# Chunks of 64 instead of 48, both batches of a chunk as one pair, and inverses of 32-row halves, in a delta-rule attention followed by two MLPs

## The chip, the cores and the metric

The kernel runs on one core of one Trainium2 chip. The metric is the device time of one execution in microseconds (us). The engines are named as the profile names them: PE is TensorE's matmul, PEld its weight load, DVE is VectorE, ACT is ScalarE, POOL is GpSimd, SP is SyncE, which here only issues DMAs. `L492` is line 492 of the kernel before.

## The reference

For each of 4 batches and 8 heads, a state of 40 x 40 runs over 768 tokens; then every token (320 values, the 8 heads side by side) goes through two MLPs. Cut to what matters:

```python
for t in range(S):                                   # 768 tokens, per batch and head
    y[t] = einsum(r[t], state)                       # read before the update
    Sa = einsum(state, a[t])
    state = state * w[t] - outer(Sa, b[t]) + outer(v[t], k[t])
x = y.transpose(...).reshape(3072, 320)
x = x / sqrt(mean(x*x) + 1e-6) * rms_g
x = (silu(x @ w_gate) * (x @ w_val)) @ w_out         # 320 -> 1536 -> 320
h = x @ w_in                                         # 320 -> 2048
out = (h - tanh(h)) @ w_out2                         # 2048 -> 320
```

## The kernel before, in words

**Attention in chunks.** The recurrence is computed in chunks of C = 48 tokens. A unit is one chunk of one batch, all 8 heads of it (as 4 x 2); there are 64 units. Units alternate between the two batches of a pair (G = 2), so two consecutive units are independent and each unit depends on the one two places before it. For each unit, in order:

- the p stage (`emit_p`): two scans and a reciprocal on DVE for the running products of w, then three multiplications on POOL (some on DVE at the start), L245 to L252. Its results go to memory (`sp`) and are loaded again as `kl` and `Q`.
- `m` (L268): the products of the chunk's a and b, evicted by ACT, stored to memory (`md`).
- the inverse of the unit triangular matrix I + M of each head: for most units in groups of 8 by `inverse`, 47 steps of a multiplication (L308) and an addition (L310), each step cut between POOL (its first rows) and DVE; for the first two groups by `inverse_halves` on 24-row halves (L335, L338), which `join_halves` puts together with three products (L369, L373, L377). The results go to memory (`td`, `th`) and come back as `tt`.
- `rhs` (L492), `u` (L506, the solve: the inverse times the right-hand side), `kb` (L447, a transpose of the next unit's keys), `d` (L519, the state's change), `ut` (L554, a transpose of u), `z` (L563, with a mask on DVE, L565), `mak` (L469) and `s` (L544, a transpose of the state), and for each pair of units `y` (L585, L587), `e` (L456, a transpose of the decay) and the RMS norm. `x2` (L607) transposes the finished rows of x.

**The MLPs.** The weights come as words of 64 bits and are split into two single-precision parts by `split_words`: per piece two instructions on ACT (L160, L167), five on DVE (L161, L162, L163, L165, L166) and two on POOL (L170, L171); 48 pieces for the first MLP (6 chunks of 8), 40 for the second. MLP 1 runs in 12 blocks of 256 tokens; each block has 12 steps f of 128 hidden columns: two `up` products of 8 matmuls (L635, gate and value), evictions on ACT and DVE, a split into a high and a low part on ACT and POOL (L662, L663), and `down` with 6 matmuls (L640 to L642). MLP 1 is mixed into the attention: between the attention's steps `moe(R * MO[i])` puts in as many pieces of MLP 1 as a credit allows (R is about 0.8 for each of 7 places in a unit), if a block's 256 tokens are done. MLP 2 follows in 6 blocks of 512 tokens with 16 steps each.

**What sets the order.** The program text gives each instruction a priority number (`step` advances it, `later` puts work behind), and a scheduler turns these into one fixed order on each engine. Every engine then works through its list in order and waits where an operand isn't there. SP issues nearly all DMAs in one list. `warm(n)` puts n bf16 matmuls without a use into the PE list. Most buffers of a unit exist twice (`NR = 2`; `RU` and `SN` three times), and the PE results rotate through three banks (`bank`).

**Start.** The first 16 units have hand-made places: MPOS, P8, JOINS, EXTRA, RATES and other tables set when their p stage, `m`, joins and the first weight pieces come.

## Time and profile before

| | |
|---|---|
| time of 3 runs, median (lowest to highest) | 1452.94 us (1450.84 to 1456.26) |
| the profiled execution's own time | 1455.73 us |
| its span in the trace | 1454.0 us |
| granted PE clock, mean over the span | 0.923 of full |
| first `rhs` (unit 0) | 65.8 us |
| first matmul of MLP 1 (L635) | 168.5 us |
| `rhs` of the last unit | 1002.0 us |
| first matmul of MLP 2 | 1081.5 us |

How to read it: the attention with MLP 1 mixed in fills the span from about 170 to 1012 us, the rest of MLP 1 and MLP 2 the time behind that. A row of a group gives the line, the engine, the tiles, the shapes and a count, then the busy time in us and the mean duration of one in ns, and behind the next bar the idle time of the engine ahead of it, with what released it. In the windows view a row is a stretch: its length, then for each engine its busy time and in brackets its number of instructions, then the granted PE clock (1.00 is full), the DMA engines' share and GB/s. The trace counts an fp32 product twice (two passes), so `x8` in the order of instructions stands as 16 in the trace; a transpose counts once.

### The profile page before, as it was taken

How to read it: one execution, taken by the hardware profiler on the slowest of the kernel's cores; microseconds unless marked ns; L12 is line 12 of the kernel's file. 1: busy time of each engine (PE TensorE's matmuls, PEld its weight loads, DVE VectorE, ACT ScalarE, POOL GpSimd, SP SyncE). 2: the span in 40 equal slices, each digit the busy share in tenths (PEclk: the TensorE clock that was granted, in tenths of full speed). 3: DMA queues.
4: the chain of work that ended last, by engine and by line, in shares of the span. 5: the costliest groups of instructions: out<-in, count | busy, mean ns of one | idle time of the engine just before them, and what ended most of it. 6: DMA issues, size and time to landing. Idle time of an engine off the chain costs nothing.

```text
span 1454.0 us, 38826 instructions
## 1 busy us (share of the span) xinstructions
PE 1310.8 (90%) x15090; PEld 1167.2 (80%) x15090; DVE 882.8 (61%) x2156; ACT 606.9 (42%) x1655; POOL 799.1 (55%) x1397
## 2 busy tenths in 40 slices
PE   2797798898998998998999989999887999999998
PEld 2676687787887888887888878899776898989988
DVE  8678898886957846845954957333869322222221
ACT  1244454443444453444445445444434433333332
POOL 6475786886855845854862864112757433333333
PEclk9976766779999999898999999999999999999999
DMA  7687576556455455455455243331322100010000
GB/s 175 144 239 181 145 192 166 153 135 145 122 135 132 117 146 137 120 135 133 107 140 118 64 120 101 81 75 49 103 76 87 35 17 18 23 35 24 1 19 19
DMA packets 224872, 151.44 MB, mean 104 GB/s; under 512 B 135600, under 2 KB 199632, under 8 KB 223920
## 3 DMA queue, kind: packets, MB, share of 16 engines
q1 hardware_dynamic: 197608, 131.96, 36.1%
q10 hardware_dynamic: 27080, 16.98, 4.2%
q8 instruction: 120, 1.97, 0.6%
q14 instruction: 64, 0.52, 0.1%
HBM read 111.23 MB, written 37.65 MB: 102 GB/s over the span
## 4 chain that ended last, share of the span: by engine, by line
PE 55%; DVE 23%; DMA 8%; POOL 6%; issue 4%; ACT 2%; SPq 1%; DVEq 0%; POOLq 0%; ACTq 0%
PE ups L635 22%; PE acc L640 6%; PE acc L642 5%; PE acc L641 5%; DVE arena L308 3%; DVE arena L310 3%; PE bank L563 2%; DVE fa L163 2%; DMA arena<-md 2%; DVE raw L166 2%; DVE fa L161 2%; PE bank L554 1%; PE gapped L519 1%; PE bank L506 1%; PE bank L469 1%
## 5 line engine op out<-in xcount | busy, mean ns | idle before, releaser
L635 PE MATMUL ups<-xh,w1c 128*128 128x256 f32 x1440 | 259.0, 313 | 16.7 <-DVE hf L659 9.1
L1152 POOL TENSOR_TENSOR hl<-th,hh 128x512 fp32r<-128x512 f32 x96 | 124.9, 1301 | 208.2 <-ACT hh L1151 203.3
L635 PEld LDWEIGHTS ups<-xh,w1c 128*128 128x128 f32 x1440 | 205.2, 204 | 29.1 <-DVE hf L659 11.1
L1148 DVE TENSOR_TENSOR th<-ups,th 128x512 f32<-128x512 f32 x96 | 66.3, 691 | 233.1 <-ACT th L1147 233.1
L663 POOL TENSOR_TENSOR hl<-hf,hh 128x256 fp32r<-128x256 f32 x144 | 117.4, 815 | 150.9 <-ACT hh L662 147.4
L635 PE MATMUL ups<-xl,w1c 128*128 128x256 f32 x864 | 158.6, 295 | 0.0
L635 PEld LDWEIGHTS ups<-xl,w1c 128*128 128x128 f32 x864 | 132.8, 204 | 0.0
L308 POOL TENSOR_TENSOR tmp<-arena 128x88 f32<-128x88 f32 (+45 forms) x282 | 108.2, 384 | 40.3 <-DMA arena<-md 23.9
L310 POOL TENSOR_TENSOR arena<-arena,tmp 128x88 f32<-128x88 f32 (+45 forms) x282 | 113.1, 401 | 16.7
L308 DVE TENSOR_TENSOR arena<-arena 128x182 f32<-128x182 f32 (+27 forms) x234 | 98.7, 422 | 32.0 <-POOL tmp L308 20.9
L1147 ACT ACTIVATE th<-ups 128x512 f32<-128x512 f32 x96 | 57.2, 596 | 130.4 <-PE ups L635 130.4
L657 DVE SCALAR_TENSOR_TENSOR th<-th,ups 128x256 f32<-128x256 f32 x144 | 59.5, 413 | 77.6 <-ACT th L656 76.8
L635 PE MATMUL ups<-yh,w2c 128*128 128x512 f32 x360 | 103.1, 397 | 2.9 <-DVE th L1148 2.9
L640 PE MATMUL acc<-w1c,hh 128*128 128x320 f32 x288 | 103.6, 360 | 0.1
L662 ACT CAST hh<-hf 128x256 fp32r<-128x256 f32 x144 | 58.4, 406 | 99.8 <-DVE hf L659 98.1
L310 DVE TENSOR_TENSOR arena<-arena 128x182 f32<-128x182 f32 (+27 forms) x234 | 93.3, 399 | 4.8
L642 PE MATMUL acc<-w1c,hl 128*128 128x320 f32 x288 | 92.6, 321 | 1.2 <-POOL hl L663 1.2
L656 ACT ACTIVATE th<-ups 128x256 f32<-128x256 f32 x144 | 55.2, 383 | 92.1 <-PE ups L635 83.2
L641 PE MATMUL acc<-w1c,hh 128*128 128x320 f32 x288 | 91.9, 319 | 0.0
L1151 ACT CAST hh<-th 128x512 fp32r<-128x512 f32 x96 | 59.5, 620 | 75.2 <-DVE th L1148 62.6
L640 PE MATMUL acc<-w2c,hh 128*128 128x320 f32 x288 | 86.9, 312 | 2.7 <-ACT hh L1151 2.7
L641 PE MATMUL acc<-w2c,hh 128*128 128x320 f32 x288 | 87.3, 312 | 0.0
(175 smaller groups left out, 3238.2 us busy)
## 6 DMA issues: line engine op xcount, KB each, us to landing
arena<-in_abkw_dram SPq DMA_DIRECT2D x48, 314.0 KB
RU<-in_vr_dram SPq DMA_DIRECT2D x64, 234.0 KB
sp<-arena ACTq DMA_DIRECT2D x40, 313.6 KB
kl<-sp SPq DMA_DIRECT2D x60, 156.0 KB
Q<-sp SPq DMA_DIRECT2D x60, 156.0 KB
raw<-in_w_out_dram SPq DMA_DIRECT2D x28, 320.0 KB
arena<-md SPq DMA_DIRECT2D x12, 576.0 KB
pl<-in_abkw_dram SPq DMA_DIRECT2D x16, 314.0 KB
```

What stands on the lines that cost most here:

```text
L308: eng.tensor_tensor(out=tv, in0=T[:, r0:r1, s:s + 1].to_broadcast([128, n, wd]), in1=M[:, s:s + 1, s + 1:C].to_broadcast([128, n, wd]), op ...
L310: eng.tensor_tensor(out=T[:, r0:r1, s + 1:C], in0=T[:, r0:r1, s + 1:C], in1=tv, op=ALU.add)
L635: PE.matmul(ps, lhsT=l, rhs=r[:, :n], start=i == 0, stop=i == 7)
L640: PE.matmul(acc[t][:, :DM], lhsT=hh[:, c], rhs=oh, start=f == 0, stop=False)
L641: PE.matmul(acc[t][:, :DM], lhsT=hh[:, c], rhs=ol, start=False, stop=False)
L642: PE.matmul(acc[t][:, :DM], lhsT=hl[:, c], rhs=oh, start=False, stop=f == nf - 1)
L657: DVE.scalar_tensor_tensor(out=th, in0=th, scalar=1.0, in1=ps[:, 0], op0=ALU.add, op1=ALU.mult)
L662: ACT.copy(hh, hf)
L663: POOL.tensor_tensor(out=hl, in0=hf, in1=hh, op=ALU.subtract)
L1148: DVE.tensor_tensor(out=th, in0=ps, in1=th, op=ALU.subtract)
L1151: ACT.copy(hh, th)
L1152: POOL.tensor_tensor(out=hl, in0=th, in1=hh, op=ALU.subtract)
```

## The change

C is 64 and the work item is a pair: both batches of one chunk, 24 pairs of 128 tokens, so that one `rhs` or `u` row of the order now has 16 products instead of 8, and a finished pair is one tile of 128 rows of x. What is different part by part:

- **Inverse.** Only the two 32-row halves on the diagonal are inverted, 31 steps each, always with one engine for a group: the first group (pairs 0, 1) on DVE, the second (2, 3), the third (4 to 7) and all later groups of four pairs on POOL. `inverse_halves`, `join_halves` and the joins' products are gone.
- **Solve.** `u` multiplies by the two inverted halves, of which the upper half is kept; `w` multiplies the upper half by the coupling block (`MX`, loaded from `md`), DVE subtracts it from the right-hand side `RS`, and `u2` multiplies again for the lower half.
- **Buffers.** One each of Q, VS, UV, RU, RS, TT, MX, EP and `kl`; `turn` rotates two PE banks beside `solve` and `gapped`.
- **Eviction and transposes.** `ut` and `s` are now products with the identity. The right-hand side is evicted half by ACT, half by DVE.
- **Weights.** `NRAW` 4 to 3, the split's scratch `fa` 4 to 2. The first two chunks of MLP 1's weights are split from the end of the first inverse on, chunks 2 to 5 after the last instruction of the third inverse.
- **MLP 1's place.** `moe(RATE)` with RATE = 2.1 at 9 places in a pair; ahead of `x2` a loop puts in what is left of the block before. Until the first block has begun, `warm(8)` stands there.
- **Output.** Each tile of 128 rows goes out in two DMAs of 64 rows.

The core of the diff:

```diff
-C = 48
+C = 64
+HC = C // 2
-GROUPS = [(0, 4), (4, 8)] + [(g, g + 8) for g in range(8, NU, 8)]
+GROUPS = [(0, 2), (2, 4)] + [(g, g + 4) for g in range(4, NP, 4)]
-NRAW = 4
+NRAW = 3
-RATE = 0.80
+RATE = 2.1
...
-        for s in range(C - 1):
-            nr, wd = s // jm + 1, C - 1 - s
-            for eng, r0, r1, buf in ((POOL, 0, min(nr, SPLIT), tmp), (DVE, SPLIT, nr, arena)):
...
+        for s in range(HC - 1):
+            nr, wd = s // jm + 1, HC - 1 - s
+            eng.tensor_tensor(out=tv, in0=T[:, :nr, s:s + 1].to_broadcast([128, nr, wd]),
                               in1=M[:, s:s + 1, s + 1:HC].to_broadcast([128, nr, wd]), op=ALU.mult)
+            lastd[0] = eng.tensor_tensor(out=T[:, :nr, s + 1:HC], in0=T[:, :nr, s + 1:HC], in1=tv, op=ALU.subtract)
...
+    def emit_u(p):
+                    PE.matmul(sol[r, w, q], lhsT=TT[r, w, q], rhs=RS[r, w, q], start=True, stop=True)
+        for s in range(2):
+            ACT.copy(UV[0:HC, :, s], sol[64 * s:64 * s + HC])
+    def emit_w(p):
+                    PE.matmul(tv[64 * s:64 * s + C, w, q], lhsT=MX[0:C, s, w, q], rhs=UV[0:C, w, s, q], start=True, stop=True)
+        DVE.tensor_tensor(out=RS, in0=RS, in1=tv, op=ALU.subtract)
+    def emit_u2(p):
+                    PE.matmul(sol[r, w, q], lhsT=TT[r, w, q], rhs=RS[r, w, q], start=True, stop=True)
+        for s in range(2):
+            ACT.copy(UV[HC:C, :, s], sol[64 * s + HC:64 * s + C])
...
+            i0 = inverse(0, DVE, M0, T0, fp)
+            i1 = inverse(1, POOL, M1, T1, fp)
+            i2 = inverse(2, POOL, M2, T2, fp)
...
+            run(i0)
+            first_w = lastd[0]
+            load_t(0)
+            emit_rhs(0)
+            warm(WARM0)
+            run(i1)
+            for u in range(12, 16):
+                emit_p(u, fp, POOL)
+                spill_p(u, SP)
+                if u % 2:
+                    emit_m(u // 2, fp)
+        with tc.issue_after(first_w.ins):
+            prep1(range(EARLY1), w1a)
+        later(2, run, i2)
+        last_t = lastd[0]
...
+        for p in range(NP + 1):
+            if p == 1:
+                with tc.issue_after(last_t.ins):
+                    prep1(range(EARLY1, KF1 // 2), w1p)
+            if now:
+                if p:
+                    emit_rhs(p)
+                    load_q(p + 1)
+            if p:
+                emit_y(p - 1)
+            moe(RATE)
+            if now:
+                emit_u(p)
+                moe(RATE)
+                emit_w(p)
+                    emit_kb(p + 1, 0)
+                moe(RATE)
+                emit_u2(p)
+                    emit_kb(p + 1, 1)
+                moe(RATE)
+                emit_d(p)
+                emit_ut(p)
+            if p:
+                while begun[0] < (p - 1) // 2 - 1 or (mlp and begun[0] == (p - 1) // 2 - 1):
+                    piece()
+                emit_x2(p - 1)
+            moe(RATE)
```

In this loop MLP 1's pieces can only come where a block's two pairs are done, and the credit and the loop put the 24 `up` products of a block where the order shows.

Three places in the order. First, PE's list around the start of the first solve. Before, with `rhs` of the first two units, the first join (L369) and, after 8 warming matmuls, `u` of unit 0:

```order
L492 MATMUL bank<-VS_209,Q_213 48x40 x8
L492 MATMUL bank<-VS_210,Q_214 48x40 x8
L369 MATMUL bank<-idn,mt 24x24 x16
...
L506 MATMUL bank<-rs_1133,arena 48x40 x8
L373 MATMUL bank<-mt 24x24 x16
```

Now `rhs` of pair 0 (L392) has 60 warming matmuls (L284) behind it, then come `m` of pairs 6 and 7 (L243), 8 warming matmuls, and `u` of pair 0 (L403):

```order
L392 MATMUL turn_137<-VS,Q 64x40 x16
L284 LDWEIGHTS wz
L284 MATMUL wps<-wz 128x256
...
L243 MATMUL turn_136<-po 64x64 x16
L243 MATMUL turn_137<-po 64x64 x16
...
L403 MATMUL solve<-RS,TT 64x40 x16
```

The `m` products of pairs 6 and 7, for which units 12 to 15 must have gone through their p stage, now stand ahead of the first solve; on POOL's list the p stage of units 12 to 15 stands behind the whole second inverse, among whose 62 instructions the POOL parts of the first 18 weight pieces are mixed.

Second, DVE's list at the same place. Before, the first masks of z (L565) alternate with the weight split (L161 to L166):

```order
L565 TENSOR_TENSOR z<-bank,msk 96x384
L161 TENSOR_SCALAR fa<-fa 128x256
L565 TENSOR_TENSOR z<-bank,msk 96x384
L162 TENSOR_SCALAR fa<-fa 128x256
L163 SCALAR_TENSOR_TENSOR fa<-raw,fa 128x256
L165 TENSOR_SCALAR raw<-fa 128x256
```

Now 18 pieces of the weight split (L138 to L143) and the p stage of units 12 to 15 stand ahead of the subtraction (L414) that pair 0's solve needs; here the end of that row:

```order
L142 TENSOR_SCALAR raw<-fa 128x256
L143 SCALAR_TENSOR_TENSOR raw<-raw 128x256
L214 SCALAR_TENSOR_TENSOR sx<-pl,z_151 104x260
L217 RECIPROCAL zr<-sx 104x4
L218 SCALAR_TENSOR_TENSOR po<-pl,zr 104x260
L214 SCALAR_TENSOR_TENSOR sx<-pl,z_151 104x260
L217 RECIPROCAL zr<-sx 104x4
L218 SCALAR_TENSOR_TENSOR po<-pl,zr 104x260
L414 TENSOR_TENSOR RS<-RS,turn_136 128x320
```

The subtraction moved behind all of these.

Third, PE's list in the steady part. Before, in a unit from `u` (L506) to `ut` (L554), with `down` and `up` of MLP 1 (L640 to L642, L635) beside them:

```order
L506 MATMUL bank<-rs,tt 48x40 x8
L447 MATMUL bank<-idn,kl 96x104 x4
L640 MATMUL acc_7539<-w1c_934,hh 128x320
L641 MATMUL acc_7539<-w1c_934,hh 128x320
L642 MATMUL acc_7539<-w1c_934,hl 128x320
L640 MATMUL acc_7540<-w1c_934,hh 128x320
L641 MATMUL acc_7540<-w1c_934,hh 128x320
L642 MATMUL acc_7540<-w1c_934,hl 128x320
L519 MATMUL gapped<-UV_211,kb 40x40 x8
L554 MATMUL bank<-idn,UV_211 40x48 x8
L635 MATMUL ups<-xh,w1c_1033 128x256 x5
```

Now, in every even pair: `u` (L403), `w` (L413), `kb` (L358), `u2` (L421), `kb`, `d` (L433), `ut` (L468), `x2` (L518), and only then `up` (L537):

```order
L403 MATMUL solve<-RS,TT 64x40 x16
L413 MATMUL turn_136<-UV,MX 64x40 x16
L358 MATMUL turn_137<-idn,kl 128x104 x4
L421 MATMUL solve<-RS,TT 64x40 x16
L358 MATMUL turn_136<-idn,kl 128x104 x4
L433 MATMUL gapped<-UV,kb 40x40 x16
L468 MATMUL turn_137<-idn,UV 40x64 x16
L518 MATMUL turn_136<-idn,XS 128x128 x3
L537 MATMUL ups<-xh,w1c_878 128x256 x5
L537 MATMUL ups<-xl,w1c_878 128x256 x3
```

In the even pairs the MLP pieces that stood between these steps are behind `x2` of the pair before it; in the odd pairs they still stand between the steps.

More of the change, by code (lines that the diff above doesn't have):

```diff
@@ L444, in emit_kb @@
+    def emit_kb(p, w):
+        bk = kl_t[p][w]
         t = bank()
@@ new lines, in wkv_chunks__then__gated_mlp__then__tanh_mlp_kernel, with some2 @@
+        todo = []
+        def some2():
+            if not w2:
+                tasks2.extend(early2())
+            with tc.issue_after(gate[0].ins), tc.issue_after(gate_act[0].ins):
+                while raw2:
+                    later(PRE2, split_words, *raw2.pop(0))
+            while tasks2 and len(raw2) < 2:
+                rows, *rest = tasks2.pop(0)
+                raw2.append((later(PRE2, fetch64, rows, rest[0]), *rest))
+        held = []
+        for p in range(NP + 1):
+            now, more, n = p < NP, p + 1 < NP, p + LOOKP
+            if p == 1:
+                for u in range(2 * KEEP):
+                    po_t.pop(u)
```

1081 lines of the change are left out of this document (404 added, 677 removed).

## The prediction, made before the changed kernel ran

> **What bounds the kernel now.** First the page: the busy time, the clock in 40 slices and the chain of work that ended last.
>
> ```profile
> PE 1310.8 (90%) x15090; PEld 1167.2 (80%) x15090; DVE 882.8 (61%) x2156; ACT 606.9 (42%) x1655; POOL 799.1 (55%) x1397
> PEclk9976766779999999898999999999999999999999
> PE 55%; DVE 23%; DMA 8%; POOL 6%; issue 4%; ACT 2%; SPq 1%; DVEq 0%; POOLq 0%; ACTq 0%
> PE ups L635 22%; PE acc L640 6%; PE acc L642 5%; PE acc L641 5%; DVE arena L308 3%; DVE arena L310 3%; PE bank L563 2%; DVE fa L163 2%; DMA arena<-md 2%; DVE raw L166 2%; DVE fa L161 2%; PE bank L554 1%; PE gapped L519 1%; PE bank L506 1%; PE bank L469 1%
> ```
>
> PE is busy for 90% of the span, but at a low clock in the first fifth, and DVE, with weight splits and inverses, holds 23% of the chain. So the span has parts with different limits; the windows view shows them (PE, PEld, DVE, ACT, POOL, then the clock).
>
> ```profile
> 0.00:60.00 60.00, 24.31 (x314) 19.83 (x315) 48.82 (x161) 8.94 (x21) 31.11 (x74) 1.00 0.71 168
> 60.00:120.00 60.00, 57.21 (x894) 47.13 (x891) 39.54 (x98) 27.82 (x76) 41.76 (x57) 0.74 0.77 201
> 240.00:300.00 60.00, 51.56 (x695) 44.91 (x695) 53.01 (x123) 26.66 (x79) 46.05 (x80) 0.70 0.54 141
> 300.00:420.00 120.00, 112.46 (x1577) 100.72 (x1577) 91.82 (x243) 51.69 (x159) 91.62 (x222) 0.92 0.54 131
> 1160.00:1278.00 118.00, 118.00 (x664) 106.40 (x663) 28.26 (x44) 42.47 (x76) 41.19 (x32) 1.00 0.08 25
> ```
>
> Until 300 us DVE has the most work that counts and PE runs at about 0.7 of its clock; then PE sets the pace. The rate of the attention comes from `rhs`, 16 records a unit: its line, and its records in two stretches.
>
> ```profile
> L492 PE MATMUL bank<-VS,Q x1024: 213/216/303, 65.8 to 1002.3; 112*48 112x40 f32 x166, 104*48 104x40 f32 x5
> 307.50:660.00 352.50, 14.28 (x400) 11.30 (x400) 0.94 0.53 131
> 660.00:1003.00 343.00, 14.87 (x416) 11.79 (x416) 0.96 0.41 101
> ```
>
> The two stretches hold 51 starts, the first at 307.5, the last at 1002: 50 steps in 694.5 us, 13.9 us a unit, or (128/48 units) 37.1 us for 128 tokens. Below, all is counted for 128 tokens, now one pair.
>
> **PE's work, before and after.** The timeline of PE at full clock gives the price of each step, from its start to the start of the next row.
>
> ```profile
> 307.50 0.56 PE L492 MATMUL bank<-VS,Q 112*48 112x40 f32 x16
> 307.99 0.86 PE L635 MATMUL ups<-xh,w1c 128*128 128x256 f32 x5
> 309.04 0.76 PE L635 MATMUL ups<-xh,w1c 128*128 128x256 f32 x5
> 310.09 0.56 PE L506 MATMUL bank<-rs,tt 48*48 48x40 f32 x16
> 310.58 0.56 PE L447 MATMUL bank<-idn,kl 104*96 104x104 f32 x4
> 310.92 0.39 PE L640 MATMUL acc<-w1c,hh 128*128 128x320 f32 x1
> 311.97 0.51 PE L519 MATMUL gapped<-UV,kb 96*40 96x40 f32 x16
> 312.40 0.52 PE L554 MATMUL bank<-idn,UV 48*40 48x48 f32 x8
> 312.85 0.86 PE L635 MATMUL ups<-xh,w1c 128*128 128x256 f32 x5
> 313.91 0.84 PE L563 MATMUL bank<-RU 104*96 104x96 f32 x8
> 314.68 0.56 PE L469 MATMUL bank<-Q,kl 40*48 40x48 f32 x16
> 315.17 0.86 PE L635 MATMUL ups<-xh,w1c 128*128 128x256 f32 x5
> 317.65 0.92 PE L268 MATMUL bank<-arena 40*48 40x48 f32 x32
> 318.51 0.57 PE L456 MATMUL bank<-idn,EP 104*112 104x104 f32 x4
> 320.39 0.29 PE L585 MATMUL bank<-SN,RU 104*48 104x40 f32 x4
> 321.96 0.86 PE L635 MATMUL ups<-xh,w1c 128*128 128x256 f32 x5
> ```
>
> Before, a unit: `rhs`, `u` and `mak` 0.49 each, `kb` 0.34, `d` 0.43, `ut` 0.45, `z` 0.77, `m` 0.86/2, half of `e` (as `kb`) 0.17, half of `y` 1.57/2; `s` and `x2`, not quoted, I put at 0.35. Sum 5.2; times 128/48 it is 13.8 us. One f of MLP 1 is two `up` of 1.05 and a `down` of 1.05, 3.15; 6 f for 128 tokens are 18.9. Together 32.7, against 37.1 measured: 4.4 us are waits and low clock.
>
> After: 32 records for 16 also in 64 columns. `m` against `u` gives 0.37 for 16 records, 8 steps with two halves side by side: 46 ns a step of 48 columns, and 0.12 a run. `z` (8 steps, 96 columns) gives 81 ns. Between them, 64 columns cost 58 ns, 128 columns (beyond `z`) 104. So `rhs`, `u`, `w`, `u2`, `mak` and `m` are 0.12 + 16 x 0.058 = 1.05 each, 6.3; `z` 2 x 0.95; `y`, 16 runs, 1.9; `kb` 2 x 0.4; `d`, `s`, `ut` (40 columns) 0.75 to 1.0 each, 2.5; `e` and `x2` 0.65. Sum 14.1: what the larger chunk saves, `w` and `u2` take again, and PE's work for 128 tokens is 2% more than before. With the MLP 33.0. The Trainium skill, "TensorE: Matmul & The Clock Gate", section on LDWEIGHTS, has a weight load at the columns divided by 1.2 in ns; 64 columns would be 53, not 58, by it and the sum 0.5 us a pair less; the 46 ns for 48 columns in the rows stand 6 above that rule.
>
> **Waits in the solve.** The chain `rhs`, `u`, `w`, subtraction, `u2`, `d`, `ut`, `x2` has no MLP product between its steps in even pairs. How that runs, a place of before without cover shows: a wait ahead of `z`, the clock behind it (the window row from 289.60 to 299.00), then unit 12's `rhs` and the first `up` behind it.
>
> ```profile
> 281.37 0.99 PE L563 MATMUL bank<-RU 104*96 104x96 f32 x8 [2.32 <-ACT RU L556]
> 289.60:299.00 9.40, 8.68 (x149) 7.78 (x148) 7.37 (x19) 4.11 (x13) 6.02 (x14) 0.50 0.54 126
> 289.61 0.87 PE L492 MATMUL bank<-VS,Q 112*48 112x40 f32 x16
> 301.56 1.44 PE L635 MATMUL ups<-xh,w1c 128*128 128x256 f32 x5 [0.33 <-ACT xh L623]
> ```
>
> After one wait of 2.32 us the clock is 0.50 although PE is then nearly always busy, and the unit from `rhs` to the next `up` takes 12 us, where the prices above give about 5.5. In after's even pair the waits are an eviction and a subtraction each between `u` and `w` (1.2), `w` and `u2` (0.5, `kb` covers the rest), `u2` and `d` (0.8), and behind `x2` its eviction (2.3): 4.8 us, an estimate from the 2.32 and 0.33 above, bounds 2 and 7. Half clock adds between 0 and 6.5 to that chain's 9 us of products (the upper end from 12 for 5.5, less the waits); no row says how much of each chain it takes, so I take the middle, 3.4. That is 8.2 every second pair, 4.1 a pair. In odd pairs MLP products stand between the steps and hide the evictions; where that cover is thin, 0.33 to 2.32 us a wait come back, and I add 0.4 a pair for it: 33.0 + 4.1 + 0.4 = 37.5.
>
> What I cost at nothing here: DVE's subtraction is 0.5 us beside a DVE that loses its share of the inverses; behind it on DVE's list wait the masks of `z` and the state's update, which the next steps of the same chain need anyway. POOL has 62 inverse instructions for four pairs, some 37 us of 150, hidden as long as `hl` (L663) isn't queued behind a burst of them (rival 3). With one buffer instead of two, TT, MX, RU and VS are loaded after their last use in the pair before, 10 to 25 us ahead of their next; uncovered, it would be a landing time of some us a pair. The two output DMAs lie under MLP 2's products but for the last.
>
> **The start.** The first instruction of the first inverse on DVE and the group it belongs to, POOL's inverse instructions and the two of a weight split, and how many of L171 ended between 158 and 266.6 us:
>
> ```profile
> 24.42 0.18 DVE L335 TENSOR_TENSOR tmph<-mt 128x23 f32<-128x23 f32 x1 [1.93 <-DMA mt<-md]
> L338 DVE TENSOR_TENSOR mt<-mt,tmph 128x22 f32<-128x22 f32 (+16 forms) x46 | 11.4, 267 | 0.7
> L310 POOL TENSOR_TENSOR arena<-arena,tmp 128x88 f32<-128x88 f32 (+45 forms) x282 | 113.1, 401 | 16.7
> L170 POOL TENSOR_TENSOR fa<-fa,w1c 128x256 f32<-128x256 f32 (+2 forms) x19 | 19.6, 1034 | 12.0 <-ACT w1c L167 7.8 <-DMA raw<-in_w_gate_dram 1.5 <-DVE fa L162 0.9
> L171 POOL TENSOR_TENSOR w1c<-fa,raw 128x256 fp32r<-128x256 f32 (+2 forms) x21 | 17.5, 834 | 2.2 <-issue 1.2
> 158.00:266.60 108.60, 26.18 (x31) 0.67 0.68 178
> ```
>
> Before, eight units are staged when the first inverse starts at 24.4, 3.05 us each. Now twelve are, of 260 elements for 196: 49 us, and SP's loads of units 6 to 11 stand behind the stores and loads of `md`: 54 (bounds 45, 60). Its 62 steps at 0.267 end at 71. On POOL, the second inverse takes 62 x 0.401 = 25 and the 18 pieces between its steps 18 x (1.034 + 0.834) = 34: 130. Units 12 to 15 and `m` of pairs 6 and 7, which PE has ahead of `u`: 16 more, four units of three multiplications and their loads. `u` of pair 0 starts at 146 and everything behind it on PE's list waits; before it came soon after the `rhs` of 65.8. SP's list has the loads of TT and MX of pair 1 behind the stores of those units, so pair 1 can't start earlier either. Pairs 0 and 1 are done near 194, at DVE's pace and without MLP; the third inverse, 62 steps of twice the elements (0.6), holds POOL to 206, and the last 30 pieces at 108.6/31 = 3.5 follow until 310 (with three buffers for raw words and two for the scratch instead of four, two pieces are still in flight, so I keep that pace). MLP block 0 needs them all, so 512 tokens and block 0 are done at 317 (bounds 295, 335). Before, unit 12 starts at 289.6 and 512 tokens are 10.67 units: 270. Lag 47.
>
> **The tail.**
>
> ```profile
> 1012.11 0.29 PE L585 MATMUL bank<-SN,RU 104*48 104x40 f32 x4
> 1081.49 1.33 PE L635 MATMUL ups<-yh,room 128*128 128x512 f32 x5
> ```
>
> From the last `y` to the end are 442 us. Before, 17 f stand behind it in the order, which took 68 us, 4.0 each; now 12. Five fewer at 3.15 to 4.0 are 16 to 20; 442 becomes 423. MLP 2 is the same.
>
> **Sum.** 317 + 20 x 37.5 + 423 = 1490 of span; before, in the same terms, 270 + 20 x 37.1 + 442 = 1454. Own time is 1.7 above the span, and the median of the runs 2.8 below the profiled run: **1489**.
>
> **Rivals.**
>
> 1. *Faster: the inverse sets before's pace.* L308, L310 and the load of `md` hold 8% of the chain, 116 us, a piece of it for each group of eight; each step is split between POOL and DVE and waits for both. Now a group's inverse is due three pairs after its `m`, some 110 us, for 37 us of POOL. If these waits were most of the 4.4 us, a pair is 33.0 plus 1.5: 317 + 690 + 423 = 1430, with a start 10 us earlier 1420. It decides below 35.4 a pair (a median of 1446). For it: the chain's 8%. Against: PE was busy for 112.46 of 120 us, and the new chain has two more waits.
> 2. *Same: the clock holds.* The Trainium skill's "TensorE: Matmul & The Clock Gate" asks, in its closing table, only that there be no PE idle of over about 3 us between bursts. The waits above are shorter than 2.4 each; if the clock stayed full, 35.8 a pair, the rows give 317 + 716 + 423 = 1456, a median of 1455. By that rule a wait of 2.32 us should not halve the clock; the rows say it did, with 0.50 behind it.
> 3. *Slower still.* Half clock over the whole even chain: 33.0 + 0.4 + (4.8 + 6.5)/2 = 39.1, and some 0.1 for POOL's inverse in bursts of ten instructions (6 us) ahead of an `hl` that `down` waits for: 39.2 a pair, 317 + 784 + 423 = 1524. For it: the 0.50 of the quoted window lasts through the whole unit. Against: MLP products follow at once and, at 307.5 and after, the clock is full again.
>
> **Chances.** Forecast 0.43, rival 3 0.20, rival 1 0.25, rival 2 0.12. A measurement of this kernel tells 0.5%, 7 us, from no change. Range 1427 to 1528: it takes in rivals 2, 3 and the nearer half of 1. The start's bounds (about 20 us either way) and those of the even chain (2 us a pair, 40 in all) reach as far. Faster 0.25, same 0.12, slower 0.63. The likeliest case's own range is 1468 to 1510.
>
> **What would show it.** Right: `u` of pair 0 at about 146 behind `m` of pairs 6 and 7; last L148 for MLP 1 near 310; in even pairs PE waits for ACT and DVE between L403 and L537 and a clock near 0.5 in them; `rhs` every 75 us per two pairs; 12 f behind the last `y`. Wrong: two pairs in under 71 us, a clock above 0.95 from 320 on, or the first `u` before 120. A start later than 335, or POOL's `hl` as what PE waits for, would speak for rival 3.

## The result and the profile after

The changed kernel takes **1543.5 us** (median of 4 runs, 1539.15 to 1545.49) against 1454.2 us for the kernel before on the same chip: a ratio of 1.061, with a 95% interval of 1.058 to 1.065. So it is slower by 6.1%, where 1489 was forecast, 2.4%. The direction was right and the size wrong, and the measured time lies 15 us above the range.

First the page of the changed kernel: busy time, the clock in 40 slices, and the chain of work that ended last by engine.

```profile
span 1543.7 us, 34820 instructions
PE 1270.9 (82%) x14396; PEld 1166.3 (76%) x14396; DVE 708.1 (46%) x1371; ACT 481.9 (31%) x1101; POOL 723.8 (47%) x1099
PEclk9965788776959796979699969998899999999999
PE 56%; DVE 17%; POOL 11%; DMA 6%; issue 4%; ACT 3%; SPq 1%; ACTq 0%; POOLq 0%; DVEq 0%
```

Every engine has less to do than before: PE 40 us less, DVE 175 less, ACT 125 less, POOL 75 less. Nevertheless the span is 90 us longer. The clock is low from the third to the tenth slice, as it was before, and now also in single 6s and 7s in the middle, which were 9s before. On the chain POOL has risen from 6% to 11%.

The windows view of the changed kernel gives the start in pieces of 60 us, and the last row the whole stretch from `rhs` of pair 4 to the last `y`. Its columns are the window and its length, the busy time of PE, PEld, DVE, ACT and POOL, then PE's clock, the DMA share and GB/s.

```profile
0.00:60.00 60.00, 11.19 (x160) 9.54 (x160) 32.81 (x54) 6.38 (x12) 24.77 (x48) 1.00 0.81 204
60.00:120.00 60.00, 17.14 (x164) 13.96 (x164) 52.20 (x130) 9.35 (x23) 38.00 (x63) 0.77 0.34 97
120.00:180.00 60.00, 21.93 (x286) 17.82 (x287) 26.67 (x48) 10.48 (x24) 38.50 (x77) 0.55 0.44 112
240.00:300.00 60.00, 40.44 (x482) 38.09 (x482) 52.95 (x111) 24.14 (x62) 38.33 (x49) 0.81 0.53 135
352.40:1113.70 761.30, 702.91 (x9941) 662.94 (x9940) 297.72 (x605) 241.75 (x590) 320.17 (x572) 0.87 0.39 99
```

The same stretch of the kernel before, from where its 512 tokens were done (270, as the prediction had it) to its last `y`, in its windows:

```profile
270.00:1012.00 742.00, 688.67 (x9710) 616.15 (x9708) 489.24 (x1274) 332.79 (x1022) 426.97 (x946) 0.93 0.47 116
```

Until 180 us PE now works for 50 us in all. Before, the first 120 us alone held 81 us of PE's work. With the prediction's own terms the times compare as follows (all from the profiled executions; the start is the moment of `rhs` of pair 4, before of the 512th token; the tail runs from the last `y` to the end):

| | start | body | tail | span |
|---|---|---|---|---|
| before | 270 | 742 (37.1 a pair) | 442 | 1454 |
| predicted | 317 | 750 (37.5) | 423 | 1490 |
| after | 352 | 761 (38.05) | 430 | 1544 |

Of the 90 us lost, 82 lie in the start and 19 in the body, and the tail gives 12 back. Of the 54 us by which the forecast was short, 35 are the start, 11 the body and 7 the tail. Since the steady stretch lost only 19 us, and PE had less work, the first question is what ends the start; the second is why the body is no faster although DVE, ACT and POOL have so much less to do in it.

**The start, read row by row.** DVE's timeline at the first inverse (L272, L274):

```profile
58.31 0.70 DVE L214 TENSOR_TENSOR_SCAN sx<-pl,z 104x260 f32<-104x260 f32 x1 [15.56 <-DMA pl<-in_abkw_dram]
62.92 0.16 DVE L272 TENSOR_TENSOR tmph<-arena 128x31 f32<-128x31 f32 x1
84.69 0.19 DVE L274 TENSOR_TENSOR arena<-arena,tmph 128x16 f32<-128x16 f32 x1
```

DVE stands idle for 15.56 us for the load of a unit's `pl`, and the first inverse then runs from 62.9 to 84.9. POOL's timeline carries on:

```profile
84.58 0.24 POOL L272 TENSOR_TENSOR tmph<-arena 128x31 f32<-128x31 f32 x1 [3.34 <-issue]
146.30 0.23 POOL L274 TENSOR_TENSOR arena<-arena,tmph 128x16 f32<-128x16 f32 x1
172.48 0.24 POOL L272 TENSOR_TENSOR tmph<-arena 128x31 f32<-128x31 f32 x1 [10.77 <-DMA arena<-md]
224.08 0.27 POOL L274 TENSOR_TENSOR arena<-arena,tmph 128x31 f32<-128x31 f32 x1
224.30 1.41 POOL L147 TENSOR_TENSOR fa<-fa,w1c 128x256 f32<-128x256 f32 x2
243.76 1.61 POOL L147 TENSOR_TENSOR fa<-fa,w1c 128x256 f32<-128x256 f32 x2 [12.30 <-ACT w1c L144]
```

The second inverse fills 84.6 to 146.5; the third waits 10.77 us for its own load of `md` and then shares POOL with p stages until 224.3; only then come the remaining 32 of the 48 weight pieces, with a hole of 12.3 us behind the third of them. The last of their L148 starts at 341.7, and `rhs` of pair 4 follows at 352.4. So the second inverse had 16 pieces between its steps and not 18: ACT and DVE were done with the 17th and the 18th at 142, and their POOL parts stood behind the third inverse until 224.3. The hole shows on ACT, which begins each piece:

```profile
239.42 0.43 ACT L137 ACTIVATE fa<-raw 128x256 f32<-128x256 f32 x1 [7.46 <-DMA raw<-in_w_val_dram]
```

Until 226 two of the three buffers for raw words were held by those two pieces, and the third by words whose piece waited for the split's scratch. SP issued the next loads from 228.9 on, behind loads for the next pairs on its list, and the DMA engines, busy at 0.95 from 229.0 to 239.4, took 10 us over the first of them.

PE's waits, of 0 to 180 us and of 180 to 352 us, give the same from the other side:

```profile
PE turn L243 <- POOL po L225: 91.5, 8, 58.7
PE turn L243 <- DVE po L224: 29.1, 8, 7.7
```

```profile
PE ups L537 <- POOL w1c L148: 25.2, 5, 6.9
```

Each line gives the total, the number of waits and the longest. In one single wait PE stands for 58.7 us ahead of `m` of pair 6, because units 12 to 15 are behind the second inverse on POOL's list; and after 180 the weight pieces are what it waits for most.

**The body.** PE's waits between 352.4 and 1113.7 us:

```profile
PE acc L542 <- ACT hh L564: 21.3, 9, 5.3
PE acc L544 <- POOL hl L565: 17.6, 14, 3.4
PE ups L537 <- ACT xh L525: 12.7, 10, 2.6
PE turn L413 <- ACT UV L405: 5.1, 10, 0.5
```

The steps of the solve, of which the forecast made so much, wait 5.1 us in all, once in each of the ten even pairs for 0.5 us (L413). The MLP's own `down` waits 38.9 us, for `hh` and `hl`. Where that happens shows PE's timeline at the end of an odd pair and in the even pair behind it:

```profile
670.11 0.42 PE L542 MATMUL acc<-w1c,hh 128*128 128x320 f32 x1 [1.50 <-ACT hh L564]
671.65 0.42 PE L544 MATMUL acc<-w1c,hl 128*128 128x320 f32 x1 [0.98 <-POOL hl L565]
672.60 1.94 PE L392 MATMUL turn<-VS,Q 128*64 128x40 f32 x32
674.33 0.42 PE L501 MATMUL turn<-sn,RU 104*64 104x40 f32 x4
680.33 2.37 PE L413 MATMUL turn<-UV,MX 64*64 64x40 f32 x32 [0.51 <-ACT UV L405]
691.34 1.43 PE L537 MATMUL ups<-xh,w1c 128*128 128x256 f32 x5 [0.94 <-ACT xh L525]
```

And the windows view of the same place: the drain, the even chain, the first `up`s, and what follows.

```profile
668.00:672.60 4.60, 2.12 (x13) 1.31 (x11) 1.58 (x3) 1.27 (x4) 3.60 (x7) 0.95 0.81 232
672.60:691.30 18.70, 17.28 (x268) 15.61 (x267) 2.84 (x6) 6.03 (x14) 1.44 (x5) 0.50 0.58 162
691.30:696.00 4.70, 4.66 (x22) 4.66 (x23) 0.98 (x2) 0.38 (x1) 0.00 (x0) 0.50 0.00 0
696.00:712.50 16.50, 16.50 (x210) 16.12 (x209) 10.02 (x19) 4.59 (x12) 7.57 (x12) 1.00 0.40 97
```

The block's pieces run out just before the odd pair ends. Its last two f have nothing beside them, so `down` waits for the casts of its own f, 2.5 of 4.6 us idle. Behind that the clock stands at 0.50 for 23.4 us, although PE is busy for 21.9 of them, and the 32 products of `rhs` take 1.73 us to the next row instead of the 1.05 that the prediction had for them at full clock.

In every fourth pair (5, 9 and 13, of 44.9, 43.4 and 42.4 us) the drain is longer. PE's timeline at the end of pair 9, and ACT's and DVE's just ahead of it:

```profile
586.70 0.41 PE L544 MATMUL acc<-w1c,hl 128*128 128x320 f32 x1 [1.52 <-POOL hl L565]
593.20 0.63 PE L542 MATMUL acc<-w1c,hh 128*128 128x320 f32 x1 [5.29 <-ACT hh L564]
```

```profile
589.37 0.34 ACTq L230 DMA_DIRECT2D sp<-arena  x1
589.81 0.42 ACT L369 COPY en<-turn 128x320 f32<-128x320 f32 x1 [4.58 <-POOL arena L225]
592.74 0.40 ACT L564 CAST hh<-hf 128x256 fp32r<-128x256 f32 x1 [2.51 <-DVE hf L561]
```

```profile
589.37 1.12 DVE L214 TENSOR_TENSOR_SCAN sx<-arena,z 104x260 f32<-104x260 f32 x1 [6.45 <-POOL arena L225]
592.28 0.42 DVE L561 SCALAR_TENSOR_TENSOR hf<-th,ups 128x256 f32<-128x256 f32 x1
```

POOL, with an inverse on its list, finishes the p stage's L225 late. Two engines stand behind it. ACT stands 4.58 us at the p stage's store (L230), but it is free again at 590.2. DVE stands 6.45 us at the next scan of the p stage (L214), and the product that makes `hf` (L561) is behind that scan on its list; ACT's cast of `hh` then waits 2.51 us for this `hf`, and `down` for the cast. So what ends last in PE's wait of 5.29 us is DVE's list, not the store. DVE waits at L214 for 7.9, 6.5 and 6.0 us in pairs 5, 9 and 13 and for more than 2.5 us in no other pair of the body.

### The profile page after: what moved, and what is told of

Read it like the earlier page. It is cut to its first block, busy times and chain, and to the rows that moved or that the text cites. A ratio compares the mean times of both kernels' runs of the same rounds, so it can differ in the third digit from the quotient of the medians.

```text
span 1543.7 us, 34820 instructions
## 1 busy us (share of the span) xinstructions
PE 1270.9 (82%) x14396; PEld 1166.3 (76%) x14396; DVE 708.1 (46%) x1371; ACT 481.9 (31%) x1101; POOL 723.8 (47%) x1099
## 4 chain that ended last, share of the span: by engine, by line
PE 56%; DVE 17%; POOL 11%; DMA 6%; issue 4%; ACT 3%; SPq 1%; ACTq 0%; POOLq 0%; DVEq 0%
PE ups L537 23%; PE acc L544 5%; PE acc L542 5%; PE acc L543 5%; POOL arena L274 3%; DVE fa L140 3%; DVE fa L138 3%; DVE fa L139 2%; PE turn L478 2%; PE turn L413 2%; DMA md<-ms 2%; POOL tmp L272 2%; DVE raw L143 2%; PE solve L421 2%; PE turn L468 2%
## 5 line engine op out<-in xcount | busy, mean ns | idle before, releaser
L537 PE MATMUL ups<-xh,w1c 128*128 128x256 f32 x1440 | 250.5, 307 | 57.0 <-POOL w1c L148 25.2
L537 PEld LDWEIGHTS ups<-xh,w1c 128*128 128x128 f32 x1440 | 212.4, 208 | 67.6 <-ACT xh L525 26.8
L565 POOL TENSOR_TENSOR hl<-hf,hh 128x256 fp32r<-128x256 f32 x144 | 109.7, 762 | 303.2 <-ACT hh L564 276.0
L537 PE MATMUL ups<-xl,w1c 128*128 128x256 f32 x864 | 159.5, 296 | 0.0
L537 PEld LDWEIGHTS ups<-xl,w1c 128*128 128x128 f32 x864 | 134.0, 206 | 0.0
L542 PE MATMUL acc<-w1c,hh 128*128 128x320 f32 x288 | 98.6, 342 | 26.2 <-ACT hh L564 26.2
L243 PE MATMUL turn<-po 40*64 40x64 f32 x256 | 17.9, 317 | 120.6 <-POOL po L225 91.5
L243 PEld LDWEIGHTS turn<-po 40*64 40x64 f32 x256 | 15.1, 218 | 123.3 <-POOL po L225 100.8
L537 PE MATMUL ups<-yh,w2c 128*128 128x512 f32 x360 | 102.7, 395 | 1.4 <-DVE th L925 1.3
L543 PE MATMUL acc<-w1c,hh 128*128 128x320 f32 x288 | 92.6, 322 | 0.0
L542 PEld LDWEIGHTS acc<-w1c,hh 128*128 128x128 f32 x288 | 57.2, 199 | 29.5 <-ACT hh L564 29.0
L272 POOL TENSOR_TENSOR tmp<-arena 128x31 f32<-128x31 f32 (+15 forms) x124 | 63.8, 514 | 29.1 <-DMA arena<-md 21.8
```

The source lines that it names most:

```text
L272: eng.tensor_tensor(out=tv, in0=T[:, :nr, s:s + 1].to_broadcast([128, nr, wd]), in1=M[:, s:s + 1, s + 1:HC].to_broadcast([128, nr, wd]), o ...
L537: PE.matmul(ps, lhsT=l, rhs=r[:, :n], start=i == 0, stop=i == 7)
L542: PE.matmul(acc[t][:, :DM], lhsT=hh[:, c], rhs=oh, start=f == 0, stop=False)
L543: PE.matmul(acc[t][:, :DM], lhsT=hh[:, c], rhs=ol, start=False, stop=False)
L565: POOL.tensor_tensor(out=hl, in0=hf, in1=hh, op=ALU.subtract)
```

## The experiments

Each is the changed kernel with the edit shown; ratios are to the kernel before, run beside it on the same chip, with their 95% intervals. "Body" is the stretch from `rhs` of pair 4 to the last `y`, 20 pairs; "start" is the time of that `rhs`.

### 1. The MLP spread over both pairs

```diff
-RATE = 2.1
+RATE = 1.7
```

> Only RATE changes, 2.1 to 1.7, so that MLP 1's pieces last through two pairs and stand between the steps of the even pair's chain too (at two of its places); the order of the start is the same. If the uncovered even chain and its half clock cost some 4 us a pair: from the rhs of pair 4 to the last y 759 us become 690 to 720, the clock there goes up, total 1490 to 1510. If the pairs are limited by something else (evictions, loads into the single buffers): that stretch stays within 10 us of 759 and the total within 10 of 1543.

1482.8 us, ratio 1.016 (1.011 to 1.021). The start is unchanged (348.9 for 352.4), the body 704.2 for 761.0. Its windows:

```profile
348.90:1053.50 704.60, 661.65 (x9937) 626.77 (x9937) 295.92 (x601) 238.55 (x589) 320.95 (x572) 0.94 0.41 105
```

The same products (9937 and 9941 records) keep PE busy for 661.65 us instead of 702.91, at a clock of 0.94 instead of 0.87, and its waits for `hh` and `hl` fall from 38.9 to 9.2 us. By the kernel's own counting a block of MLP 1 costs 12 x (2 x 0.87 + 0.82) = 30.7 of credit, and the 18 places of two pairs give 37.8 at 2.1 and 30.6 at 1.7. So with 1.7 some of the block is left when the odd pair ends, and an `up` can stand ahead of the even pair's `u`. Nearly 57 us of the changed kernel's body were thus not its attention, but where its MLP pieces stand. The body came out as expected; the total, with its start and tail unchanged, 7 us below the 1490 to 1510 expected. Pairs 7 and 8, in a row and without a drain, took 31.3 and 35.3 us here.

### 2. Units 12 to 15 behind the first solve

```diff
-            for u in range(12, 16):
-                ...
-                if u % 2:
-                    emit_m(u // 2, fp)
...
+                else:
+                    for u in range(12, 16):
+                        ...
+                        if u % 2:
+                            emit_m(u // 2, fp)
+                    next(i2)
+                    next(i2)
+                    later(2, run, i2)
```

The third inverse moves with them.

> The p stage of units 12 to 15, m of pairs 6 and 7 and the third inverse are put behind the solve of pair 0 in the text, so that the first solve no longer waits for them; the rate is as in the changed kernel. If the late first solve sets the start: the first u comes at about 90 to 95 instead of 164, the rhs of pair 4 60 us earlier, total about 1480. If the weight pieces behind the third inverse set it: the first u is as early, but the last piece of MLP 1's weights and the rhs of pair 4 stay within 15 us of 342 and 352, and the total within 15 us of 1543.

1515.2 us, 1.039 (1.032 to 1.046). `u` of pair 0 starts at 100.9 instead of 164.0, 63 us earlier; `rhs` of pair 4 only 19 earlier, at 333.0, and the last weight piece 19 earlier, at 322.8. So the wait of 58.7 us, the longest in the kernel, was worth a third of its length: behind it stood another chain, and the start ends with the weight pieces, not with the first solve. (The total fell by 28; the body came out 12 us shorter as well.) The last piece moved by a little more than the 15 us that the second branch allowed. The trace shows where: the last step of the third inverse comes at 225.5, near the 224.1 of the changed kernel, but the pieces behind it start 3 us apart, without the hole of 12.3. The loads of their raw words, issued at 227.8, land within 3 us, with the DMA engines busy at 0.57 instead of 0.95.

### 3. The first weight pieces behind the second inverse

```diff
-        with tc.issue_after(first_w.ins):
+        with tc.issue_after(last_m.ins):
             prep1(range(EARLY1), w1a)
```

> The first 18 weight pieces may only start behind the second inverse, not among its steps. The second inverse then ends near 112 and the first u comes near 130 instead of 164; the pieces lose 30 us of POOL. If the first solve sets the start: 30 us less in total. If the weight pieces set it: last piece at 350 or later, rhs of pair 4 at 355 to 375, total 1545 to 1565.

1533.3 us, 1.051 (1.045 to 1.057). `u` of pair 0 comes 33 us earlier, as the POOL time of those pieces gives; but `rhs` of pair 4 didn't come later for it, it came at 336.7, 16 earlier. The expectation held in its first half only. The pieces, all put off, end earlier (326.5): the last step of the third inverse comes at 217.7 instead of 224.1, and here too the hole behind it is missing: the next loads of raw words, issued at 220.0, land within 3 us at a DMA share of 0.60.

### 4. The second inverse on DVE

```diff
-            i1 = inverse(1, POOL, M1, T1, fp)
+            i1 = inverse(1, DVE, M1, T1, fp)
```

> The second inverse (62 instructions, 25 us on POOL) is done by DVE as the first one, about 17 us there; POOL keeps the weight pieces. If POOL's list is what ends the start: last piece 20 to 25 us earlier, rhs of pair 4 at about 330, total about 1520. If DVE's share of the splits is: the 17 us come on top there, the last piece is within 5 us of 342 and the total unchanged.

1534.6 us, 1.051 (1.044 to 1.058): start 337.7 for 352.4, the first `u` at 149.6. The last piece comes 15 us earlier, at 326.9, where 20 to 25 were expected. POOL's share of the start is real, and it is worth 15 us of it; the body came out 12 us longer, 772.9, so that the total gained only 9.

### 5. Warming products in the even chain

```diff
-            if not done and begun[0] < 1:
+            if not done:
                 warm(WARM)
-                step(1.0)
+                step(1.0 if begun[0] < 1 else 0.0)
```

Eight products of no use stand at each place of the even chain that has no MLP piece, 320 in all.

> The changed kernel with 8 warming matmuls (about 0.85 us) at each of the four uncovered places of an even pair's chain; nothing else is moved. If a good half of the even pair's loss is the half clock behind the short waits: the clock from pair 4 to the last y goes from about 0.85 to over 0.95 and the stretch of 761 us becomes 725 to 740, total 1505 to 1525. If the loss is waits alone: the clock matters little, the warming matmuls only lie in the waits or add to them, the stretch stays at 755 to 775, total 1540 to 1560.

1541.4 us, 1.058 (1.055 to 1.060), the changed kernel's time. Its windows for the body:

```profile
355.50:1120.50 765.00, 709.59 (x10262) 661.82 (x10262) 297.50 (x606) 241.74 (x591) 320.83 (x572) 0.92 0.38 99
```

The clock rises from 0.87 to 0.92 and the body stays at 765 us. The 40 groups of 8 take 1.04 us at full clock and 1.89 at half; in all they keep PE busy for 52.9 us, and the products that count for 46 less than before. From `rhs` to `x2` five of the ten even pairs take 12.6 us at a clock of 1.00, where 16.9 at 0.50 was typical, the other five 15.7 to 20.0 at 0.59 to 0.78. The drain ahead of these chains stays: PE's waits for `hh` and `hl` are 37.1 us (38.9 without the groups). So idle work cured the low clock in half of the chains, and nothing was gained; work that has to be done anyway, in the same places (experiment 1), gains 57.

### 6. The later inverses further back on POOL's list

RATE 1.7, and of each later inverse all but the two first steps are put 12 places of the planner's priority further back.

```diff
-                        later(T_LATE, run, held.pop(0))
+                        late = held.pop(0)
+                        later(T_LATE, lambda: (next(late), next(late)))
+                        later(T_LATE + 12, run, late)
```

> RATE 1.7 as in the run with that rate, and the later inverses' instructions stand 12 units of priority behind their loads instead of straight behind them. With RATE 1.7 every fourth pair (6, 10, 14, 18) takes 42 to 46 us instead of 31 to 35. If that is POOL waiting some 10 us for the inverse's load with the p stage and ACT's store of it queued behind: those pairs fall to 34 to 37, the stretch from pair 4 to the last y from 704 to 670 to 680, total 1450 to 1460. If it is POOL's work itself (37 us of inverse in one pair): they stay above 40 and the total within 8 us of 1483.

1485.5 us, 1.019 (1.015 to 1.023), no other than experiment 1. It was to shorten the pairs that had become the slow ones there, 6, 10 and 14 with 42.7, 45.7 and 43.2 us where the others take 30 to 38; it left them at 42.8, 46.1 and 45.1, since POOL's list hardly moved. As a test of the cause it says nothing. What happens there shows in experiment 1's own trace, pair 10: POOL is late once more, and here the store on ACT, waiting twice as long, is what PE feels. POOL's timeline, then ACT's, then PE's:

```profile
548.32 0.24 POOL L272 TENSOR_TENSOR tmp<-arena 128x31 f32<-128x31 f32 x1 [10.43 <-DMA MX<-md]
566.40 0.68 POOL L225 TENSOR_TENSOR arena<-arena,sx 104x256 f32<-104x256 f32 x1
```

```profile
567.11 0.35 ACTq L230 DMA_DIRECT2D sp<-arena  x1
567.56 0.43 ACT L369 COPY en<-turn 128x320 f32<-128x320 f32 x1 [9.77 <-POOL arena L225]
```

```profile
562.68 1.13 PE L392 MATMUL turn<-VS,Q 128*64 128x40 f32 x32
568.03 0.44 PE L501 MATMUL turn<-sn,RU 104*64 104x40 f32 x4 [4.23 <-ACT en L369]
568.27 0.42 PE L503 MATMUL turn<-kb,z 128*64 128x40 f32 x4
```

The head of the inverse waits on POOL for its load, the p stage comes late behind it, the store of the p stage (L230) stands on ACT's list and holds ACT for 9.77 us, and the copy of `en` behind that store lets PE's `y` wait 4.23 us. DVE stands 9.16 us for the same L225 at its L214. The windows of that pair and the next:

```profile
562.70:608.40 45.70, 39.27 (x512) 36.50 (x511) 18.27 (x33) 12.78 (x31) 36.04 (x66) 0.78 0.40 110
608.40:638.40 30.00, 30.00 (x454) 28.79 (x453) 15.10 (x30) 10.31 (x25) 10.82 (x18) 1.00 0.50 131
```

36 us of POOL in a pair of 45.7 us at a clock of 0.78, against 10.8 in one of 30.0 at full clock.

### 7. Weight pieces no longer behind the third inverse

RATE 1.7, and the 32 later pieces are held only until the second inverse is done; the third inverse takes its scratch from another pool, so that they don't share buffers.

```diff
-            i2 = inverse(2, POOL, M2, T2, fp)
+            i2 = inverse(2, POOL, M2, T2)
...
-                with tc.issue_after(last_t.ins):
+                with tc.issue_after(last_m.ins):
                     prep1(range(EARLY1, KF1 // 2), w1p)
```

> RATE 1.7, and the weight pieces of chunks 2 to 5 need not wait for the end of the third inverse: POOL's list then has both side by side (the inverse's scratch is taken from another pool for that). If the start is ended by the weight pieces held behind the third inverse: last piece near 310 instead of 350, rhs of pair 4 near 310 to 320, total 1445 to 1460. If POOL's total work ends it, the same work is only mixed otherwise: last piece and pair 4 within 10 us of 350, total 1475 to 1490.

1448.0 us, 0.995 (0.993 to 0.996). Against experiment 1 the last piece comes 33 us earlier, at 318.1, and `rhs` of pair 4 24 earlier, at 324.6, while `u` of pair 0 stays at 163.6. It is the counterpart of experiment 2: there the first solve moved by 63 and the start by 19; here the first solve did not move and the start did by 24. (The body came out 14 us shorter as well.) What ends the start is the pieces, and what held them was their place behind the third inverse on POOL's list, not the amount of POOL's work: the third inverse, now among the pieces, has its last step at 311.5 instead of 221.1.

### 8 to 11. Together, and the slow pairs

Experiment 8 has the edits of 1, 2, 6 and 7.

> RATE 1.7, the later inverses behind their loads, the pieces not held behind the third inverse, and the p stage of units 12 to 15 and m of pairs 6 and 7 behind the first solve. If the parts add up: start (rhs of pair 4) at 295 to 310, 670 to 680 from there to the last y, tail 430: 1400 to 1420, faster than the kernel before. If they draw on the same slack: 1430 to 1455.

1430.9 us, 0.983 (0.981 to 0.985); start 304.2, body 693.3. The two start edits add up: 304.2 is 45 before experiment 1, 19 and 24 apart. The body is not the 670 to 680 expected, which relied on experiment 6's edit.

Experiment 9 takes the stores of the p stage off ACT in it:

```diff
-                spill_p(u, ACT if u > 24 else SP)
+                spill_p(u, SP)
```

> The run with all three start edits and RATE 1.7, with the stores of the p stage on SP's list instead of ACT's (all units). In pairs 6, 10, 14, 18 ACT stood 9.8 us at such a store (the wait is shown at the eviction of e behind it), and y waited for that eviction. If that wait is what makes these pairs 42 to 46 us: they fall below 38, the stretch from pair 4 to the last y from 693 to 660 to 670, total 1400 to 1410. If POOL's inverse itself does it, or SP's loads now stand behind the stores instead: they stay above 40, or other pairs grow, total 1420 to 1450.

1434.2 us, 0.985 (0.980 to 0.989); body 702.1, and the pairs 6, 10, 14 and 18 stay slow (47.7, 41.8, 44.8, 42.1). ACT isn't held at the store any more, yet POOL is still late, so the store is not what makes these pairs slow. DVE's list is left, here in pair 6:

```profile
376.77 1.22 DVE L214 TENSOR_TENSOR_SCAN sx<-arena,z 104x260 f32<-104x260 f32 x1 [9.14 <-POOL arena L225]
```

The next `hf` is behind this scan, ACT's cast of `hh` waits 10.08 us for it, ACT's half of the right-hand side is behind the cast, and PE's `u` waits 3.80 us for that.

Experiment 10 is experiment 8 with each later inverse handed out three steps at a time over about two pairs, instead of as a whole:

```diff
+            for _ in range(3 if spread and wait[0] < 0 else 0):
+                ...
+                        if next(spread[0], 1):
+                            spread.pop(0)
...
-                        later(T_LATE, run, held.pop(0))
+                        spread.append(held.pop(0))
```

> The run with all three start edits and RATE 1.7, with each later inverse's instructions given out three steps at a time over some two pairs, the first of them most of a pair behind its load; the stores stay on ACT. If the bunched inverse on POOL (36 us of 43 in such a pair, and a wait of 10.8 us for its load at its head) is the cause: pairs 6, 10, 14, 18 fall below 38 and no other grows by more than 2, total 1400 to 1412. If it is the store on ACT whatever POOL does: above 40, total within 8 us of 1431.

1422.4 us, 0.975 (0.970 to 0.980); body 688.4, slow pairs 41.2, 38.5, 40.7, 42.5, between its two branches. DVE's waits at L214 are at most 2.3 us now. Experiment 11 has both, the spread inverses and the stores on SP.

> Both: the inverse spread out and the stores on SP. If the two are one cause (POOL late, ACT held by it), this is within 6 us of the better of the two; if they are two, it is better by 8 us or more than each.

**1417.4 us, 0.975 (0.969 to 0.980)**, with experiment 10 the fastest: start 302.2, body 680.9 (34.0 a pair), tail 431.7; slow pairs 40.7, 38.5, 36.4, 42.1. Its windows for the body:

```profile
302.20:983.50 681.30, 647.74 (x9937) 613.99 (x9937) 295.77 (x600) 238.98 (x588) 323.62 (x575) 0.95 0.44 110
```

It is 5 us from experiment 10, within the 6 that its expectation gave to one cause. Spreading the inverses helps (1417 against 1434 with the stores on SP, on the same chip), but these pairs don't come down to the 30 to 35 us of most others. That POOL's bunched inverse costs something is shown. Much of the rest is low clock: in pairs 6, 10 and 18 PE is busy for 37.4, 36.8 and 37.3 us at 0.83, 0.82 and 0.80, in pair 14, of 36.4 us, for 32.5 at 1.00. What starts the low clock there stays open.

### 12. Without the coupling of the halves

This kernel leaves out a part of the computation: `w`, its subtraction and `u2`, so the two 32-row halves of a chunk are solved as if they did not bear on each other. RATE is 2.1 as in the changed kernel.

```diff
-            ACT.copy(UV[0:HC, :, s], sol[64 * s:64 * s + HC])
+            ACT.copy(UV[0:C, :, s], sol[64 * s:64 * s + C])
...
-                emit_w(p)
...
-                emit_u2(p)
```

> The changed kernel without w, the subtraction and u2: the lower half of u is taken from the first product, so the coupling of the halves is left out of the computation. By the forecast's terms: two products of 1.05 us on PE in every pair and 1.7 us of waits in every second, some 3 us a pair; from pair 4 to the last y 761 becomes about 700, total about 1480. If the solve's extra steps lie in waits that are there anyway: less than 1 us a pair, total above 1520.

1464.1 us, 1.006 (1.003 to 1.010). The body is 691.9 for 761.0, so the coupling costs 69 us, 3.5 a pair; from `rhs` to `x2` an even pair takes 11.8 us (16.9 with it) and an odd one 16.1 (18.5). The start, 341.8, is 11 shorter. Of the 69 us, 67 are time in which PE is busy (636.3 for 702.9), 3.3 a pair for two products that cost 2.1 at full clock; the waits that went with them were 5.1 us in all. So, at this RATE, the step that makes chunks of 64 possible takes nearly all that lies between the changed kernel and the kernel before. Without the coupling and with RATE 1.7 together was not tried.

## Why the prediction was wrong, and where it was right

**The start failed, and with it the sum.** The term was 317 with bounds of 295 and 335; it measured 352. The order of events was the one named: the first inverse after twelve units, the second on POOL with pieces between its steps, `m` of pairs 6 and 7 ahead of the first `u`, the third inverse, the pieces. What failed was adding up these terms by work alone, with no wait for a load at the joints: not at the first inverse, and not at the pieces, of which the prediction says that three buffers for raw words keep the pace:

- First inverse: 54 to 71 predicted, 62.9 to 84.9 measured. The bound of 60 was too small for a load that DVE waited 15.56 us for; SP issued it at 51.6, behind the load of `md` and what follows it on SP's list; and the 62 steps took 22 us rather than 17, with other work between them.
- Second inverse with 18 pieces: 59 us predicted, 62 measured, with 16 of them. Its beginning was late, and so the first `u`, at 164.0 for 146.
- From there to the end of the third inverse: 76 us predicted (130 to 206), 78 measured (146.5 to 224.3). This agreement is luck. The terms named in the prediction, 16 for units 12 to 15 and 37 for the inverse, give 53, and the other 23 have no row; measured are 15 for the units, a wait of 10.77 for `md` that the sum did not have, and 52 for the inverse with p stages among its steps.
- The pieces: 3.5 us each was right, but from 243.8 on; ahead of that three of them and the hole of 12.3, in which ACT waits for raw words. The prediction had it that with three buffers two pieces stay in flight; behind the third inverse none was, since all three were held, and the next loads took 10 us. The end at 310 became 342. Experiments 2 and 3, in which the hole is missing, end the pieces 19 and 15 us earlier.

Late by 9, 5, 3, 2 and 13 us, 32 in all: each stretch came out within 5 us, one of them by luck, and 22 of the 32 are two joints, the wait for a load and the hole, at which the sum had nothing. `rhs` of pair 4 then came 11 us behind the last piece, where 7 was taken. Experiments 2, 7 and 8 show that it is this last chain that counts: of the 63 us by which the first `u` can come earlier, two thirds bring nothing.

**PE's work a pair** was put at 33.0, and 2% above that of before. The runs put it lower: pairs 7 and 8 of experiment 11, at full clock, took 31.3 and 33.8 us, of which PE was busy for 31.3 and 31.9, so 31.6 a pair. In the whole program PE is busy for 40 us less than before, 6 of them warming products, and at a lower clock, so the change does save PE work. Experiment 12 shows what takes part of it again: 3.3 us of busy PE a pair for the coupling at the clock it had, of which the forecast had two products of 1.05.

**The body's size was right, its make-up only in part.** 37.5 against 38.05 a pair looks like a hit. The forecast had 33.0 of work, 1.7 of low clock (3.4 in every second pair) and 2.8 of waits (4.8 in every second, and 0.4). Measured are 35.1 of busy PE, so at least 3.5 of low clock above 31.6 of work, and 2.9 of waits. The work was too large, the low clock half of what it was, the waits right in size and wrong in place. The even chain, which was to wait 4.8 us, waits 1.8 (12.7 and 5.1 us over ten of them): where a wait was forecast, the evictions have gone by when PE, at half clock, gets there, or `y` and `kb` stand between. Half clock costs it more than 3.4: seven of the ten chains run at 0.50 to 0.53 and take 16.3 to 16.9 us from `rhs` to `x2`, the two in which the clock stayed full (16 and 20) 10.6; so 6.3, near the end of 6.5 that rival 3 took, and the first `up`s behind them run at 0.50 too. What the forecast had taken for covered, at 0.4 a pair, is the end of the MLP block in the odd pair: 38.9 of the body's 57.6 us of waits, 1.9 a pair. The cause, which experiment 1 shows: a credit of 2.1 a step uses the block up early, its drain idles PE, and the long chain behind it has nothing that brings the clock back.

**The tail** was 430 for 423: the 12 f behind the last `y` took 55.4 us to the first product of MLP 2, 4.6 each, where 3.15 to 4.0 was taken. Before, 17 f took 69.4, 4.1 each. PE is idle for 12 us of the stretch, for 10 before, so its idle time did not shrink with the f. DVE, with the splits of the next weights, is busy for 47.6 of these 55 us, and `hf` from DVE is what PE waits for most there (5.0 us, and 9.1 before). That the splits set this length is likely; no run here tests it.

**The rivals.** Rival 2, that the clock holds, fell: the windows above show 0.50 for 23.4 us behind waits of 1.50 and 0.98. By the closing table of the Trainium skill's "TensorE: Matmul & The Clock Gate" gaps of under about 3 us between bursts should not have done that; the trace differs, as it did before the change. Rival 3 had the body right in kind, half clock through the whole even chain in seven of ten pairs, but not its 39.2 a pair. Its POOL bursts exist, and cost more than the 0.1 it gave them: by way of `hl`, as it said, 1.5 us in the place shown, and by way of the p stage's scan on DVE's list another 5.29. A start later than 335, one of the signs named for it, came too, but its own sum had the start at 317. Rival 1 fell for the kernel as it was made. With the MLP spread and the start untied the attention takes 34.0 us a pair, under the 35.4 at which rival 1 was to decide, and the kernel is 2.5% faster than before. Whether for the reason it gave, that waits for the inverse set the pace before, no run here tests; and POOL's inverse still makes DVE wait.

## What to carry to other kernels

When a chain of stages is summed, the joints need a term of their own: here two of them added 9 and 12 us. Ask too what holds the buffers that the next stage needs: here two pieces waiting on POOL held up the loads of all behind them. The longest wait of a start is not its price; ask what chain ends last without it, and test by freeing each alone. And when independent work is used to cover a serial chain, deal it out so that some is left for the chain's end: one constant that did this was worth 57 us, where idle products in the same places were worth nothing. And when a wait names one engine, look at what that engine waited for itself: the store looked like the cause, and moving it changed nothing.

## What the runs showed of the hardware

- The clock falls after little and returns late. 2.5 us of idle in 4.6 were followed by half clock for 23.4 us in which PE was busy for 21.9; it came back 4.7 us after the first `up` (128 rows and 128 columns of weights, 256 columns of data), not during the 18.7 us of small products of 40 to 128 columns ahead of it. The Trainium skill's "TensorE: Matmul & The Clock Gate", Part 1, gives a sustained window of about 3.4 us for the return; the 4.7 behind the first `up` are near it, while the 18.7 us ahead of it, which the profile also counts as busy, did not do it. Whether it is the gaps between such small products or their size, no run here tells.
- Products put in only to keep the clock up raised it from 0.87 to 0.92 and changed the time by nothing that was measured (1.058 against 1.061 of before, intervals overlapping).
- ACT, issuing a store, held everything behind it on its list until what was to be stored was there: 9.77 us for one DMA issue in experiment 1 (4.58 in the changed kernel), seen only as a wait of the copy that followed it. DVE did the same at a scan whose buffer POOL still used: 6.45 us in the changed kernel.
